# Attention with a soft mixture of experts: the guard of the row sums moved from VectorE into TensorE's accumulation

## The chip, the cores and the metric

The kernel runs on one core of a Trainium2 chip. Its engines are named as in the profile: PE (TensorE, with PEld for its weight loads), DVE (VectorE), ACT (ScalarE), POOL (GpSimd) and SP (SyncE, which issues the transfers). The metric is the device time of one execution in microseconds (us), the median of several runs.

## The reference

Four batches, eight heads, 768 positions, 64 values a head. Attention looks at the first 8 keys (global) and at a causal window of 96; a slope of its own for each head, times the distance, is subtracted. What follows is a soft mixture of eight experts with four slots each.

```python
scores = q @ k^T / 8 - slope[h] * dist          # masked to global or local keys
a = exp(scores - max); a = a / (a.sum(-1) + 1e-9)
x = (a @ v) as 3072 rows of 512
logits = x @ phi                                # 32 slots
d = softmax(logits over rows);  slot_input = d^T @ x
slot_out[e] = relu(slot_input[e] @ w1[e]) @ w2[e]
out = softmax(logits over slots) @ slot_out
```

## The kernel before, in words

The attention runs in 16 units (batch and pair of heads, i = 0 and 1 within the pair). The queries of a head are cut into seven blocks of 120, the last with 48. For a unit the steps are these, each named in the code:

- `scores` (PE, three parts) makes the scores of both heads in PSUM, fp32, keys on the partitions; `biased` (DVE, three parts) adds the bias table, writes the tile `tb` and keeps a running maximum `mx`.
- `max_t` (PE) turns that maximum, `max_r` (DVE) reduces it to `nb`; `exponential` (ACT) makes `exp(tb + nb)` in place.
- `w_hi` (ACT) rounds the weights to 16 bits into `ph`, `w_lo` (POOL, now and then DVE) puts what is left over beside them. `v_hi` (POOL or ACT) and `v_lo` (DVE) do the same for the values; `v_hi` has a further column of constants, so that column 64 of each block's product is the row sum.
- `values` (PE) multiplies: 39 products of 64 or 65 columns for a head, all into one PSUM bank `x`, seven blocks of 65 columns side by side. The first of the 39 starts the accumulation, the last ends it.
- `ev_sums` (DVE) adds a small guard `eps` to the 14 row sums of both heads and writes them into `rsall`; `ev_recs` (DVE) takes their reciprocals into `rc`; `ev_mul` (DVE, one for each head) multiplies the values by them into `xn` and so frees the bank. In `eps`, rows of the last block that hold no query have 1e30, so that their reciprocal is next to nothing. For the last unit `ev_sum` and `ev_rec` do this for one head.
- `tr` (PE) and `tr_copy` (ACT, sometimes DVE) turn the result, `logits` and the `strip_` steps, `by_token` and `dispatch` take it into the mixture of experts as the units come in, and every batch's sum into `sacc`.

The order of all steps is one list written out, `ORDER`, which every engine follows for its own instructions: an engine whose next instruction waits does nothing else meanwhile. The loads of the expert weights are steps of this list as well (`piece`, `extra`, `free`); SP issues them.

Ahead of the list stand constants: six filler products on PE, the first part of a bias table (`BiasTable`, POOL and DVE), memsets on POOL (`ones`, `v`, `ph`, `lsb`, `shift`, `eps`). The list then begins with loads, `bcast` (DVE casts the two sizes `nraw` to `nf`, PE spreads them over the partitions with `ones`), `keys` and the `table_` steps (DVE, later ACT), six fillers (`warm`, products of 512 columns whose result nobody reads) and the first `scores`.

Behind the list come the last dispatch, the experts' two layers (`hidden`, `project`) and the combination with its output, whose products PE does one after the other. Beside them `check_inputs` (DVE) tests among other things that the smallest row sum in `rsall` is large enough; if a test fails, a slow general version runs.

Of the kernel before, what the change touches and what calls it, by code (L numbers as in the profile page):

```python
# [10 lines left out]
F32 = mybir.dt.float32  # L11
# [12 lines left out]
KB = 120  # L24
P = 128
NJ = 7
# [28 lines left out]
NT = B * NJ  # L55
SW = 2 * KB
NEG = -1.0e30
V_SC = 2.0 ** 6
P_EXP = 15
RS_MIN = 2.0 ** (P_EXP + 6 - 10)  # L60
RS_EPS = 1.0e-9 * RS_MIN
X_MIN = 2.0 ** -9


T_SC = 0.125
TAB_UNIT = 0.5 / T_SC

# [233 lines left out]
def tile_attention_moe(ctx: ExitStack, tc: tile.TileContext, qk, v, phi, w1, w2, nn, out):  # L301
# [120 lines left out]
    def extra(i):  # L422
        if extras:
            k, c0, c1 = extras.pop(0)
            load_w([k], c0, c1)

    sacc = ap.tile([P, DM], F32, name="sacc")
    nraw = keep.tile([1, 4], I32, name="nraw")
    nc.scalar.dma_start(out=nraw, in_=nn)

    def load_phis(u):
        nc.sync.dma_start(out=phis, in_=phi)


    lnat = keep.tile([KB, 8 * B, NS], F32, name="lnat")
    xmax = keep.tile([KB, B * H], F32, name="xmax")
    rsall = keep.tile([KB, B * H, NJ], F32, name="rsall")
    state = keep.tile([P, 16], F32, name="state")
    sl = keep.tile([P, Moe.SL], F32, name="sl")
    lsb = ap.tile([P, SW], F32, name="lsb")  # L440
    ex = ap.tile([P, SW], F32, name="ex")
    i4 = keep.tile([P, NS], F32, name="i4")
    by_row = keep.tile([P, NS], F32, name="by_row")
    ones = keep.tile([P, P], F32, name="ones")

    def blocks(w):
        return w[:, 0:6 * PB].rearrange("p (s c) -> p s c", c=PB)


    wp = psm.tile([P, 512], F32, name="wp", tag="m")  # L450
    busy_in = nc.const_aps.tensor(1.0, [P, 512], BF16)
    for _ in range(WARM):
        nc.tensor.matmul(out=wp[0:1], lhsT=busy_in[:, 0:1], rhs=busy_in, start=True, stop=True)

    table = BiasTable(nc, tabs, xn01)
    nf = keep.tile([1, 4], F32, name="nf")
    nlt = keep.tile([P, 2], F32, name="nlt")
    nc.gpsimd.memset(ones, 1.0)
    make_identity(nc, ident)
    for i in range(2):  # L460
        nc.gpsimd.memset(vhi[i][:, :, :, D:D + 1], V_SC)
        for w in (phi_[i], plo_[i]):
            nc.gpsimd.memset(blocks(w)[:, :, QW:], 0.0)
            nc.gpsimd.memset(w[:, 6 * PB:], 0.0)
    nc.gpsimd.memset(lsb[96:128, :], NEG)

    def late_constants():
        nc.gpsimd.tensor_tensor(out=i4, in0=ident[:, 0:32], in1=ident[:, 32:64], op=ALU.add)
        nc.gpsimd.tensor_tensor(out=i4, in0=i4, in1=ident[:, 64:96], op=ALU.add)
        nc.gpsimd.tensor_tensor(out=i4, in0=i4, in1=ident[:, 96:128], op=ALU.add)  # L470
        nc.gpsimd.tensor_copy(out=by_row.rearrange("p (s j) -> p s j", s=4), in_=ident.rearrange("p (s r) -> p s r", s=4)[:, :, 0:NS // 4])
        nc.gpsimd.memset(sl, 0.0)
        moe.constants()

    shift = keep.tile([P, 1], F32, name="shift")
    nc.gpsimd.memset(shift, -P_EXP * float(np.log(2.0)) / T_SC)


    eps = keep.tile([KB, NJ], F32, name="eps")
    nc.gpsimd.memset(eps, RS_EPS)
    nc.gpsimd.memset(eps[:, NJ - 1:NJ], 1.0e30)
    nc.gpsimd.memset(eps[0:TN[6], NJ - 1:NJ], RS_EPS)
    nc.scalar.activation(out=state[0:1, 4:5], in_=nc.const_aps.tensor(1.0, [1, 1], F32), func=AF.Exp)


    sc = [pss.tile([P, 2, 512], F32, name=f"sc{k}", tag=f"sc{k}") for k in range(2)]
    xx = psx.tile([P, 2, 512], F32, name="x", tag="x")
    mxs, nbs, rcs, ms = {}, {}, {}, {}  # L490

    def tb(u):
        return tbuf[u % 3]
# [111 lines left out]
    def values(u, i):  # L605
        ph, pl = phi_[i], plo_[i]
        vh, vl = vhi[u % 2], vlo[u % 2]
        x = sums(u, i)
        ops = []
        for t in range(NJ):  # L610
            for j, c in ((t, PCOL[t]), (t - 1, PCOL[t - 1] + KB)):
                if j >= 0:
                    for w, vv, d in ((ph, vh, D + 1), (ph, vl, D), (pl, vh, D + 1)):
                        ops.append((t, c, w, vv, j, d))
        for z, (t, c, w, vv, j, d) in enumerate(ops):
            nc.tensor.matmul(out=x[:, (D + 1) * t:(D + 1) * t + d], lhsT=w[:, c:c + P], rhs=vv[:, j, i, 0:d],  # L616
                             start=(z == 0), stop=(z == len(ops) - 1), skip_group_check=True)

    xv = xx[0:KB, :, 0:NJ * (D + 1)].rearrange("p i (t d) -> p i t d", d=D + 1)

    def by_query(u, i):
        return sums(u, i)[0:KB, 0:NJ * (D + 1)].rearrange("p (t d) -> p t d", d=D + 1)

    def ev_sum(u, i):
        nc.vector.tensor_tensor(out=rsall[:, 2 * u + i, :], in0=by_query(u, i)[:, :, D], in1=eps, op=ALU.add)

    def ev_rec(u, i):
        rcs[u, i] = wk.tile([KB, NJ], F32, name="rc", tag="rc", bufs=3)
        nc.vector.reciprocal(out=rcs[u, i], in_=rsall[:, 2 * u + i, :])

    def ev_sums(u):
        nc.vector.tensor_tensor(out=rsall[:, 2 * u:2 * u + 2, :], in0=xv[:, :, :, D], in1=eps.unsqueeze(1).to_broadcast([KB, 2, NJ]), op=ALU.add)

    def ev_recs(u):
        rc = wk.tile([KB, 2, NJ], F32, name="rc", tag="rc", bufs=3)
        for i in range(2):
            rcs[u, i] = rc[:, i]
        nc.vector.reciprocal(out=rc, in_=rsall[:, 2 * u:2 * u + 2, :])

    def ev_mul(u, i):  # L640
        b, p = units[u]
        c = D * (2 * (p % 2) + i)
        m = 2 * u + i
        nc.vector.tensor_tensor_reduce(  # L644
            out=xnb[(u // 2) % 3][:, :, c:c + D], in0=by_query(u, i)[:, :, 0:D], in1=rcs.pop((u, i)).unsqueeze(2).to_broadcast([KB, NJ, D]), scale=1.0,
            scalar=-3.0e38, op0=ALU.mult, op1=ALU.max, accum_out=xmax[:, m:m + 1])
# [225 lines left out]
    def table_rest_act(u):  # L872
        table.rest(nc.scalar.copy)

    def table_pair_act(p):
        table.pair_act(p)

    def table_pair(p):
        table.pair(p)

    steps = dict(piece=piece_of, free=free, extra=extra, load_phis=load_phis, bcast=bcast, keys=keys, table_rest=table_rest, table_rest_act=table_rest_act, table_pair_act=table_pair_act, warm_x=warm_x, warm=warm,
                 table_even=table_even, table_odd=table_odd, table_pair=table_pair, load_qk=load_qk, load_v=load_v, v_hi=v_hi, v_hi_act=v_hi_act, v_hi_dve=v_hi_dve, v_lo=v_lo,
                 scores=scores, biased=biased, max_t=max_t, max_r=max_r, exponential=exponential, w_hi=w_hi, w_lo=w_lo, w_lo_dve=w_lo_dve, w_hi_dve=w_hi_dve,
                 values=values, ev_sum=ev_sum, ev_rec=ev_rec, ev_sums=ev_sums, ev_recs=ev_recs, ev_mul=ev_mul, tr=tr, tr_copy=tr_copy, tr_copy_dve=tr_copy_dve,
                 logits=logits, logits2=logits2, logits_half=logits_half, logits_all=logits_all, strip_max=strip_max, strip_exp=strip_exp,
                 strip_sum=strip_sum, by_token=by_token, by_token_copy=by_token_copy, lnat_copy=lnat_copy, dispatch=dispatch, dispatch_sum=dispatch_sum)
    late_constants()
    for name, u, *args in ORDER:
        steps[name](u, *args)
    left = LeftBanks()  # L890
    put_rest = last_dispatch(left, lambda: warm_x(last))
    att.close()


    tail = ExitStack()
    ts = tail.enter_context(tc.tile_pool(name="ts", bufs=1))
# [10 lines left out]
    def check_inputs():  # L907

        def reduced(c, rows, x, axes, at_least):
            nc.vector.tensor_reduce(out=fl[0:rows, c:c + 1], in_=x, axis=axes, op=ALU.min)  # L910
            nc.vector.tensor_scalar(out=fl[0:rows, c:c + 1], in0=fl[0:rows, c:c + 1], scalar1=at_least, scalar2=None, op0=ALU.is_ge)

        reduced(1, KB, rsall[:, :, 0:6], AX.XY, RS_MIN)
        reduced(6, TN[6], rsall[0:TN[6], :, 6], AX.X, RS_MIN)
        xt = left.tile([P, 512], F32, name="xt", tag="x")
        nc.tensor.transpose(out=xt[0:B * H, 0:KB], in_=xmax, identity=ident[0:KB, 0:KB])
        nc.vector.tensor_reduce(out=fl[0:B * H, 5:6], in_=xt[0:B * H, 0:KB], axis=AX.X, op=ALU.max)
        nc.vector.tensor_scalar(out=fl[0:B * H, 5:6], in0=fl[0:B * H, 5:6], scalar1=X_MIN, scalar2=None, op0=ALU.is_ge)
        reduced(7, KB, cst[:, :, 1], AX.X, 0.5)
# [300 lines left out]
```

## Time and profile before

| | us |
|---|---|
| median of three runs | 184.98 (184.78 to 185.03) |
| profiled execution | 185.42 |
| its span, first to last instruction | 183.3 |
| busy: PE, DVE, ACT, POOL | 170.7, 141.4, 125.7, 97.2 |

The profile is of one execution. Matmuls are pipelined and their ends are modelled, so a busy PE is not PE at its peak. A row of the timeline merges like instructions in sequence: start in us from the span's beginning, duration in us, engine, line, operation, output<-inputs, shape of one, count, and in brackets the idle time before it with what ended it. A row of the waits reads: engine, tile and line that waited, what it waited for, us in total, times, longest. A row on groups has busy us and mean ns of one behind the bar.

### The profile page before, as it was taken

What the parts mean: (1) busy time and instruction counts of PE and PEld (TensorE: products, weight loads), DVE (VectorE), ACT (ScalarE), POOL (GpSimd) and SP (SyncE); (2) the same over time, 40 slices, a digit from 0 to 9 for tenths busy, and PEclk for the clock granted to TensorE, in tenths of its full rate; (3) what the DMA queues carried; (4) which work ended last, traced back from release to release, by engine and by line L of the source; (5) the groups of instructions that cost most, each with busy time, mean ns of one, the idle gap of its engine ahead of it and who ended that gap; (6) DMA issues with size and microseconds to landing.
All of it is one profiled execution on the core that took longest, in us unless ns stands there. A gap on an engine that the chain in (4) does not pass through costs nothing.

```text
span 183.3 us, 6741 instructions
## 1 busy us (share of the span) xinstructions
PE 170.7 (93%) x2805; PEld 125.8 (69%) x2805; DVE 141.4 (77%) x376; ACT 125.7 (69%) x162; POOL 97.2 (53%) x129
## 2 busy tenths in 40 slices
PE   8999899999999999999999998999899999999720
PEld 2476789787878877979888986875533256778520
DVE  5899999999998989899999999987867303345430
ACT  3489989999989999988999999953302120344320
POOL 6925689859799498797998996750010000000000
PEclk9999999999999999999999999999999999999985
DMA  5999999968999956689887399999999999989792
GB/s 191 418 407 384 398 370 384 366 229 306 414 330 353 405 154 256 230 325 382 297 326 272 87 323 384 396 356 418 415 401 407 411 401 406 370 307 401 294 368 65
DMA packets 15306, 61.41 MB, mean 335 GB/s; under 512 B 1698, under 2 KB 2850, under 8 KB 13474
## 3 DMA queue, kind: packets, MB, share of 16 engines
q1 hardware_dynamic: 15264, 60.89, 87.9%
q8 instruction: 24, 0.39, 0.9%
q14 instruction: 16, 0.13, 0.2%
q10 hardware_dynamic: 2, 0.00, 0.0%
HBM read 54.59 MB, written 6.29 MB: 332 GB/s over the span
## 4 chain that ended last, share of the span: by engine, by line


## 5 line engine op out<-in xcount | busy, mean ns | idle before, releaser
L599 POOL TENSOR_TENSOR ph<-tb,ph 128x432 f16<-128x432 f32 x83 | 85.8, 1064 | 19.5 <-ACT ph L592 18.3
L589 ACT ACTIVATE tb<-tb,nb 128x1296 f32<-128x1296 f32 x32 | 43.7, 1375 | 1.4 <-DVE nb L585 1.4
L616 PEld LDWEIGHTS <-ph 128*128 128x128 f16 x1248 | 40.7, 97 | 4.2 <-issue 2.8
L592 ACT CAST ph<-tb 128x1296 f16<-128x1296 f32 x32 | 40.6, 1272 | 2.8 <-PE x L616 0.9
L616 PE MATMUL x<-v,ph 128*128 128x65 f16 (+1 forms) x1209 | 42.0, 193 | 0.4 <-POOL ph L599 0.2
L564 PE MATMUL sc<-raw 64*128 64x216 f32 (+1 forms) x392 | 40.9, 340 | 0.0
L564 PEld LDWEIGHTS sc<-raw 64*128 64x128 f32 x392 | 32.3, 186 | 6.3 <-issue 3.8
L644 DVE CUSTOM_DVE_ANT_1 xn<-x,rc 120x448 f32<-120x448 f32 x31 | 18.3, 622 | 2.1 <-PE m L767 1.7
L573 DVE CUSTOM_DVE_ANT_1 tb<-sc,tt,mx 128x864 f32<-128x864 f32 x16 | 17.8, 1114 | 1.1 <-DVE mx L573 0.5
L542 DVE SCALAR_TENSOR_TENSOR v<-vt,v 128x896 f16<-128x896 f32 x14 | 16.2, 1160 | 0.0
L656 PE MATMUL m<-ident,xn 120*128 120x120 f32 x98 | 14.7, 276 | 0.2 <-DVE state L737 0.2
L656 PEld LDWEIGHTS m<-ident,xn 120*128 120x128 f32 x98 | 10.0, 141 | 2.7 <-issue 1.5
L101 PE MATMUL hp<-wp,sl 128*32 128x512 f32 x80 | 10.9, 595 | 0.3 <-ACT sl L96 0.3
L599 DVE TENSOR_TENSOR ph<-tb,ph 128x432 f16<-128x432 f32 x13 | 9.6, 766 | 0.0
L208 PE MATMUL cp<-sos,ct 32*128 32x128 f32 (+1 forms) x116 | 8.2, 332 | 1.3 <-DVE sos L195 1.1
L573 DVE CUSTOM_DVE_ANT_1 tb<-sc,xtt,mx 128x864 f32<-128x864 f32 x8 | 8.9, 1115 | 0.4 <-DVE mx L573 0.2
L573 DVE CUSTOM_DVE_ANT_1 tb<-sc,xta,mx 128x864 f32<-128x864 f32 x8 | 8.9, 1111 | 0.2
L573 DVE CUSTOM_DVE_ANT_1 tb<-sc,tt 128x864 f32<-128x864 f32 x8 | 8.4, 1052 | 0.5 <-PE sc L564 0.4
L535 ACT ACTIVATE v<-vt 128x896 f16<-128x896 f32 x9 | 8.6, 952 | 0.1
L156 PE MATMUL o<-wp,ht 128*32 128x128 f32 x256 | 8.2, 275 | 0.0
L156 PEld LDWEIGHTS o<-wp,ht 128*32 128x32 f32 x256 | 6.6, 110 | 1.4 <-issue 1.0
L903 POOL MEMSET ht<- 128x536 f32 x1 | 0.5, 547 | 13.1 <-PE ld L841 13.1
(235 smaller groups left out, 284.6 us busy)
## 6 DMA issues: line engine op xcount, KB each, us to landing
raw<-in_qk_dram SPq DMA_DIRECT2D x14, 832.0 KB, 5.8
wp<-in_w_dram SPq DMA_DIRECT2D x10, 1024.0 KB, 8.3
wp<-in_w_dram SPq DMA_DIRECT2D x15, 512.0 KB, 9.0
vt<-in_v_dram SPq DMA_DIRECT2D x14, 448.0 KB, 5.2
tb<-in_w_dram SPq DMA_DIRECT2D x3, 1024.0 KB, 7.8
wp<-in_qk_dram SPq DMA_DIRECT2D x2, 832.0 KB, 9.5
raw<-in_w_dram SPq DMA_DIRECT2D x2, 832.0 KB, 4.6
ph<-in_w_dram SPq DMA_DIRECT2D x2, 768.0 KB, 9.6
```

Source lines behind the costliest of these rows:

```text
L101: self.nc.tensor.matmul(out=hp[n][32 * s:32 * s + 32, :], lhsT=slv(a, c, s), rhs=w1(4 * a + s, c // 2)[:, (c % 2) * DF + 512 * n:(c % 2) * ...
L156: nc.tensor.matmul(out=o[32 * s:32 * s + 32, o0:o0 + w], lhsT=ht[:, k:k + 32], rhs=w2(4 * a + s, half)[:, at:at + w], start=(a == 0 and c ...
L535: nc.scalar.activation(out=vhi[u % 2][:, :, :, 0:D], in_=vraws(u), func=AF.Copy, scale=V_SC)
L542: nc.vector.scalar_tensor_tensor(out=vlo[k].rearrange("p j i d -> p (j i) d"), in0=vraws(u).rearrange("p j i d -> p (j i) d"), scalar=V_SC ...
L564: nc.tensor.matmul(out=z[:, i, at:at + n], lhsT=r_[r, KCOL[j]:KCOL[j] + KR], rhs=r_[r, KW + KB * j:KW + KB * j + n], start=True, stop=True)
L573: nc.vector.tensor_tensor_reduce(out=tb(u)[:, :, BW * k:BW * k + BW], in0=sc[(3 * u + k) % 2][:, :, 0:BW], in1=table.unit(u % NP, k), scal ...
L589: nc.scalar.activation(out=t, in_=t, func=AF.Exp, bias=nbs[u], scale=T_SC)
L592: nc.scalar.copy(out=blocks(phi_[i])[:, :, 0:QW], in_=tb(u)[:, i].rearrange("p (s c) -> p s c", c=QW))
L599: (engine or nc.gpsimd).tensor_tensor(out=blocks(plo_[i])[:, c, 0:QW], in0=tb(u)[:, i].rearrange("p (s c) -> p s c", c=QW)[:, c], in1=bloc ...
L616: nc.tensor.matmul(out=x[:, (D + 1) * t:(D + 1) * t + d], lhsT=w[:, c:c + P], rhs=vv[:, j, i, 0:d], start=(z == 0), stop=(z == len(ops) - ...
L644: nc.vector.tensor_tensor_reduce(out=xnb[(u // 2) % 3][:, :, c:c + D], in0=by_query(u, i)[:, :, 0:D], in1=rcs.pop((u, i)).unsqueeze(2).to_ ...
L656: nc.tensor.transpose(out=m[:, at:at + KB], in_=xnb[(u // 2) % 3][:, t, P * (p % 2):P * (p % 2) + P], identity=ident[0:KB, 0:KB])
```

## The change

The guard is added by PE: after the first of a head's 39 products a further product goes into the same accumulation. Its weights `eps_to` (128x128, bf16) are ones, its moving operand `eps_of` (128x7, bf16) holds the guard as a sum of three bf16 numbers in rows 0, 32 and 64; row 96 holds 1e30 for the last block, with zeros in `eps_to` where that block has queries. Both tiles are made by seven memsets on DVE, in place of three on POOL for `eps`. `ev_sums` and `ev_sum` go; the reciprocals are taken from PSUM into `recs`, which stays for the test at the end: the largest reciprocal against a bound in place of the smallest sum.

```diff
-ORDER = [... ('piece', 4), ('ev_sums', 0), ('ev_recs', 0), ('max_t', 2), ('biased', 3, 0), ...
+ORDER = [... ('piece', 4), ('ev_recs', 0), ('max_t', 2), ('biased', 3, 0), ...
...
+def in_parts(x, n):
+    parts = []
+    for _ in range(n):
+        bits = np.float32(x).view(np.uint32)
+        parts.append(float((bits & np.uint32(0xffff0000)).view(np.float32)))
+        x = float(np.float32(x - parts[-1]))
+    return parts
+
+RS_EPS_PARTS = in_parts(float(np.float32(RS_EPS)), 3)
...
-    rsall = keep.tile([KB, B * H, NJ], F32, name="rsall")
+    recs = keep.tile([KB, B * H, NJ], F32, name="recs")
...
     nc.gpsimd.memset(ones, 1.0)
+    eps_to = keep.tile([P, P], BF16, name="eps_to")
+    eps_of = keep.tile([P, NJ], BF16, name="eps_of")
+    nc.vector.memset(eps_to, 1.0)
+    nc.vector.memset(eps_to[96:97, 0:TN[6]], 0.0)
+    nc.vector.memset(eps_of, 0.0)
+    for k, part in enumerate(RS_EPS_PARTS):
+        nc.vector.memset(eps_of[32 * k:32 * k + 1], part)
+    nc.vector.memset(eps_of[96:97, NJ - 1:NJ], 1.0e30)
     make_identity(nc, ident)
...
-    eps = keep.tile([KB, NJ], F32, name="eps")
-    nc.gpsimd.memset(eps, RS_EPS)
-    nc.gpsimd.memset(eps[:, NJ - 1:NJ], 1.0e30)
-    nc.gpsimd.memset(eps[0:TN[6], NJ - 1:NJ], RS_EPS)
...
             nc.tensor.matmul(out=x[:, (D + 1) * t:(D + 1) * t + d], lhsT=w[:, c:c + P], rhs=vv[:, j, i, 0:d],
                              start=(z == 0), stop=(z == len(ops) - 1), skip_group_check=True)
+            if z == 0:
+                nc.tensor.matmul(out=x[:, 0:NJ * (D + 1)].rearrange("p (t d) -> p t d", d=D + 1)[:, :, D], lhsT=eps_to, rhs=eps_of,
+                                 start=False, stop=False, skip_group_check=True)
...
-    def ev_sum(u, i):
-        nc.vector.tensor_tensor(out=rsall[:, 2 * u + i, :], in0=by_query(u, i)[:, :, D], in1=eps, op=ALU.add)
-
     def ev_rec(u, i):
-        rcs[u, i] = wk.tile([KB, NJ], F32, name="rc", tag="rc", bufs=3)
-        nc.vector.reciprocal(out=rcs[u, i], in_=rsall[:, 2 * u + i, :])
-
-    def ev_sums(u):
-        nc.vector.tensor_tensor(out=rsall[:, 2 * u:2 * u + 2, :], in0=xv[:, :, :, D], in1=eps.unsqueeze(1).to_broadcast([KB, 2, NJ]), op=ALU.add)
+        nc.vector.reciprocal(out=recs[:, 2 * u + i, :], in_=by_query(u, i)[:, :, D])
 
     def ev_recs(u):
...
-        nc.vector.reciprocal(out=rc, in_=rsall[:, 2 * u:2 * u + 2, :])
+        nc.vector.reciprocal(out=recs[:, 2 * u:2 * u + 2, :], in_=xv[:, :, :, D])
...
-        reduced(1, KB, rsall[:, :, 0:6], AX.XY, RS_MIN)
-        reduced(6, TN[6], rsall[0:TN[6], :, 6], AX.X, RS_MIN)
+        reduced(1, KB, recs[:, :, 0:6], AX.XY, 1.0 / RS_MIN, ALU.max, ALU.is_le)
+        reduced(6, TN[6], recs[0:TN[6], :, 6], AX.X, 1.0 / RS_MIN, ALU.max, ALU.is_le)
```

Apart from the fifteen `ev_sums` and the two `ev_sum` taken out, `ORDER` is the same list.

## Rows read from the trace of the kernel before

**Rows 1.** Busy time by stage, 40 to 60: PE, PEld, DVE, ACT, POOL (instructions).
```profile
40.00:60.00 20.00, 19.96 (x331) 16.43 (x329) 18.96 (x50) 18.80 (x22) 16.89 (x17) 1.00 0.94 353
```

**Rows 2.** Waits of PE, 8 to 118 us: total, times, longest.
```profile
PE m L580 <- DVE mx L573: 0.6, 1, 0.6
PE m L580 <- ACT xtt L661: 0.4, 1, 0.4
PE m L656 <- DVE state L737: 0.2, 1, 0.2
PE x L616 <- POOL ph L599: 0.2, 1, 0.2
```

**Rows 3.** Timeline of PE, groups of value products and what follows one.
```profile
33.60 1.36 PE L616 MATMUL x<-v,ph 128*128 128x65 f16 x39
34.80 0.30 PE L580 MATMUL m<-ident,mx 128*128 128x128 f32 x1
...
109.27 2.52 PE L616 MATMUL x<-v,ph 128*128 128x65 f16 x78
```

**Rows 4.** Timeline of DVE at the start: cast, sizes, first bias.
```profile
3.10 0.34 DVE L852 CAST nf<-nraw 1x4 f32<-1x4 int32 x1
4.18 0.16 DVE L858 TENSOR_SCALAR nlt<-m 128x2 f32<-128x2 f32 x1 [0.74 <-PE m L854]
...
7.67 1.06 DVE L573 CUSTOM_DVE_ANT_1 tb<-sc,tt 128x864 f32<-128x864 f32 x1 [0.42 <-PE sc L564]
```

**Rows 5.** Timeline of DVE at 22 us; of PE, two groups of scores.
```profile
21.95 0.16 DVE L632 TENSOR_TENSOR rsall<-x,eps 120x14 f32<-120x14 f32 x1
22.15 0.24 DVE L638 RECIPROCAL rc<-rsall 120x14 f32<-120x14 f32 x1
...
22.34 2.10 PE L564 MATMUL sc<-wp 64*128 64x216 f32 x20
...
84.97 1.87 PE L564 MATMUL sc<-raw 64*128 64x216 f32 x20
```

**Rows 6.** Timeline of POOL and PE, three places with a wait.
```profile
76.96 1.01 POOL L532 TENSOR_SCALAR v<-vt 128x896 f16<-128x896 f32 x1 [1.03 <-PE x L616]
...
97.37 0.65 PE L616 MATMUL x<-v,ph 128*128 128x65 f16 x16 [0.17 <-POOL ph L599]
...
111.88 0.94 POOL L532 TENSOR_SCALAR v<-vt 128x896 f16<-128x896 f32 x1 [1.79 <-PE x L616]
```

**Rows 7.** Groups of instructions of DVE: the sums with their guard.
```profile
L632 DVE TENSOR_TENSOR rsall<-x,eps 120x14 f32<-120x14 f32 x15 | 2.5, 167 | 0.6 <-PE x L616 0.4
```

**Rows 8.** Timeline of DVE and PE, last unit's evaluation and transpose.
```profile
124.40 0.62 DVE L644 CUSTOM_DVE_ANT_1 xn<-x,rc 120x448 f32<-120x448 f32 x1
...
125.52 0.63 PE L656 MATMUL x<-ident,xn 120*128 120x120 f32 x4
```

**Rows 9.** Timeline of PE, short products; L841's durations (ns, min/median/max).
```profile
131.96 0.61 PE L841 MATMUL ld<-zi,sacc 128*128 128x32 f32 x4
...
L841 PE MATMUL ld<-zi,sacc x8: 276/276/297, 132.0 to 134.2; 128*128 128x32 f32 x8
```

**Rows 10.** Timeline of POOL and PE: constant, broadcast, fillers early and later.
```profile
3.23 0.20 POOL L458 MEMSET ones<- 128x128 f32 x1
...
3.59 0.55 PE L854 MATMUL m<-nf,ones 1*128 1x4 f32 x2
4.07 2.62 PE L553 MATMUL x<-const-bfloat16-1.0 128*1 128x512 bf16 x6
...
13.41 1.25 PE L553 MATMUL x<-const-bfloat16-1.0 128*1 128x512 bf16 x5
```

**Rows 11.** Timeline of DVE, short operations.
```profile
134.72 0.07 DVE L935 MEMSET fl<- 128x12 f32 x1
...
153.15 0.14 DVE L921 TENSOR_SCALAR fl<-nv 128x1 f32<-128x1 f32 x1
153.21 0.14 DVE L922 TENSOR_SCALAR fl<-nv 128x1 f32<-128x1 f32 x1
```

More of the change, by code (lines that the diff above doesn't have):

```diff
@@ L489, in tile_attention_moe @@
     xx = psx.tile([P, 2, 512], F32, name="x", tag="x")
-    mxs, nbs, rcs, ms = {}, {}, {}, {}
+    mxs, nbs, ms = {}, {}, {}
     def tb(u):
@@ L622, in by_query @@
         return sums(u, i)[0:KB, 0:NJ * (D + 1)].rearrange("p (t d) -> p t d", d=D + 1)
-    def ev_sum(u, i):
-        nc.vector.tensor_tensor(out=rsall[:, 2 * u + i, :], in0=by_query(u, i)[:, :, D], in1=eps, op=ALU.add)
     def ev_rec(u, i):
-        rcs[u, i] = wk.tile([KB, NJ], F32, name="rc", tag="rc", bufs=3)
-        nc.vector.reciprocal(out=rcs[u, i], in_=rsall[:, 2 * u + i, :])
-    def ev_sums(u):
-        nc.vector.tensor_tensor(out=rsall[:, 2 * u:2 * u + 2, :], in0=xv[:, :, :, D], in1=eps.unsqueeze(1).to_broadcast([KB, 2, NJ]), op=ALU.add)
+        nc.vector.reciprocal(out=recs[:, 2 * u + i, :], in_=by_query(u, i)[:, :, D])
     def ev_recs(u):
-        rc = wk.tile([KB, 2, NJ], F32, name="rc", tag="rc", bufs=3)
-        for i in range(2):
-            rcs[u, i] = rc[:, i]
-        nc.vector.reciprocal(out=rc, in_=rsall[:, 2 * u:2 * u + 2, :])
+        nc.vector.reciprocal(out=recs[:, 2 * u:2 * u + 2, :], in_=xv[:, :, :, D])
     def ev_mul(u, i):
@@ L644, in ev_mul @@
         nc.vector.tensor_tensor_reduce(
-            out=xnb[(u // 2) % 3][:, :, c:c + D], in0=by_query(u, i)[:, :, 0:D], in1=rcs.pop((u, i)).unsqueeze(2).to_broadcast([KB, NJ, D]), scale=1.0,
+            out=xnb[(u // 2) % 3][:, :, c:c + D], in0=by_query(u, i)[:, :, 0:D], in1=recs[:, 2 * u + i].unsqueeze(2).to_broadcast([KB, NJ, D]), scale=1.0,
             scalar=-3.0e38, op0=ALU.mult, op1=ALU.max, accum_out=xmax[:, m:m + 1])
@@ L883, in tile_attention_moe @@
                  scores=scores, biased=biased, max_t=max_t, max_r=max_r, exponential=exponential, w_hi=w_hi, w_lo=w_lo, w_lo_dve=w_lo_dve, w_hi_dve=w_hi_dve,
-                 values=values, ev_sum=ev_sum, ev_rec=ev_rec, ev_sums=ev_sums, ev_recs=ev_recs, ev_mul=ev_mul, tr=tr, tr_copy=tr_copy, tr_copy_dve=tr_copy_dve,
+                 values=values, ev_rec=ev_rec, ev_recs=ev_recs, ev_mul=ev_mul, tr=tr, tr_copy=tr_copy, tr_copy_dve=tr_copy_dve,
                  logits=logits, logits2=logits2, logits_half=logits_half, logits_all=logits_all, strip_max=strip_max, strip_exp=strip_exp,
@@ L907, in check_inputs, with reduced @@
     def check_inputs():
-        def reduced(c, rows, x, axes, at_least):
-            nc.vector.tensor_reduce(out=fl[0:rows, c:c + 1], in_=x, axis=axes, op=ALU.min)
-            nc.vector.tensor_scalar(out=fl[0:rows, c:c + 1], in0=fl[0:rows, c:c + 1], scalar1=at_least, scalar2=None, op0=ALU.is_ge)
-        reduced(1, KB, rsall[:, :, 0:6], AX.XY, RS_MIN)
-        reduced(6, TN[6], rsall[0:TN[6], :, 6], AX.X, RS_MIN)
+        def reduced(c, rows, x, axes, bound, low=ALU.min, within=ALU.is_ge):
+            nc.vector.tensor_reduce(out=fl[0:rows, c:c + 1], in_=x, axis=axes, op=low)
+            nc.vector.tensor_scalar(out=fl[0:rows, c:c + 1], in0=fl[0:rows, c:c + 1], scalar1=bound, scalar2=None, op0=within)
+        reduced(1, KB, recs[:, :, 0:6], AX.XY, 1.0 / RS_MIN, ALU.max, ALU.is_le)
+        reduced(6, TN[6], recs[0:TN[6], :, 6], AX.X, 1.0 / RS_MIN, ALU.max, ALU.is_le)
         xt = left.tile([P, 512], F32, name="xt", tag="x")
```

2 lines of the change are left out of this document (1 added, 1 removed).

## The prediction

> **What bounds the kernel now.** I read the busy time by stage first. In 40 to 60 us PE, DVE, ACT and POOL are all above 16.8 of 20 us, PE's matmul row at 19.96, DVE at 18.96, ACT at 18.80 [rows 1]; busy shares alone name no bound. So I read who waits. Between 8 and 118 us PE waits four times, 1.4 us in all: 0.6 and 0.2 for DVE, 0.4 for ACT, 0.2 for POOL [rows 2]. The timeline of PE says the same from the other side: a head's 39 value products start at 33.60 and take 1.36, the next instruction starts at 34.80, inside the modelled end of the group [rows 3]. A busy matmul is not a matmul at its peak, but its start times aren't modelled: 78 products take 2.52 us where 39 take 1.36, so one pair of weight load and product costs (2.52 - 1.36)/39 = 0.030 us, in every group, with no gap between groups. From about 24 us to 77 us I therefore take PE to set the pace, with DVE close behind but not ahead.
>
> Other stretches are set by other engines, and I followed the waits from place to place. Before 22 us it is DVE: it begins the first bias at 7.67 after 0.42 of idle [rows 4] and then runs almost without a gap to 21.95, and the longest of PE's waits, 0.6 in front of the maximum's transpose at 22.08, is for it [rows 2]. At 76.96 POOL's conversion has waited 1.03 for PE's values, POOL then holds up ACT, and PE itself stops for POOL at 97.37 [rows 6]: from 77 to 97 the path runs over POOL and ACT. From 97.4 it is PE again until POOL, at 111.88, has waited 1.79 for its values [rows 6]. After that the path goes POOL, PE, ACT, PE, DVE into the mixture of experts, whose products follow one another on PE to the end; what is late at 127 us is late at the end.
>
> **The sums and their guard on DVE.** The fifteen `ev_sums` cost 0.167 each, 2.5 in all [rows 7]; with the gap to the dependent reciprocal each takes 0.20 of DVE's time (21.95 to 22.15 [rows 5]). Two `ev_sum` of the last unit, no longer than these, go as well: 17 x 0.20 = 3.4 us less for DVE. The reciprocal now reads the accumulator itself. `ev_sums` reads the same accumulator and eps in 0.167, so I put the reciprocal's change at nothing, with 0.1 each (1.7, hidden as far as DVE has the 3.4 to give) as the upper bound. Where does the 3.4 arrive? Only where someone waits for DVE just behind an `ev_sums`. That is one place: unit 0's, at 21.95, stands in front of `biased(3,0)`, and the 20 score products at 22.34 take 2.10 where 20 elsewhere (84.97) take 1.87 [rows 5]. That 0.2 comes back. In the last unit the product `ev_mul(15,0)` starts on DVE at 124.40 and takes 0.62, but PE transposes it only at 125.52 [rows 8], behind other products in its queue: 0.5 us of slack, so both `ev_sum` there are worth nothing. Bounds: 0 to 0.6 (three such places).
>
> **The guard on PE.** Each of 32 heads gets one weight load of 128x128 16-bit values and one product of seven columns. No row has this pair. The nearest is the value product itself, with a weight load of the same size: 0.030 [rows 3]. From below it could be next to nothing, if load and product slip in beside their neighbours; from above, four fp32 products of 32 columns with 128x128 fp32 weights take 0.61 where one lasts 0.276, so (0.61 - 0.276)/3 = 0.11 apiece [rows 9]. I take 0.030, since both operands are 16-bit and the columns are fewer than 64. Not all 32 are on the path: unit 0's two lie before PE's wait at 22.08; units 1 to 8 are 16 heads in the stretch 24 to 77; the next six fall where PE waits for POOL and ACT; about four count in 97 to 112; in the last units the added product is second in a group that then waits anyway. So 20 x 0.030 = 0.6 us (0 to 2.2 by the bounds).
>
> [...]
>
> **The constants at the start.** Three POOL memsets go, into the shade of POOL's other constants. Seven DVE memsets come, and where they stand counts: in program order behind the bias table's first part and ahead of the cast of `nf`. That cast starts at 3.10 and takes 0.34 [rows 4]; `ones` on POOL ends at 3.23 + 0.20; PE's broadcast starts at 3.59 [rows 10]. So both operands are there at 3.43 and 3.44: the cast has no slack. Behind it wait the broadcast, then six fillers on PE in order (4.07 + 2.62), the first scores, and on DVE, from 4.18, the rest of the bias table [rows 4, 10]. Everything up to the DVE-paced stretch moves by what the memsets take. A memset lasts 0.07 [rows 11]; independent small operations start 0.06 apart (153.15, 153.21 [rows 11]); one that must wait for its predecessor's write starts 0.20 behind it, as the reciprocal does. Two of the seven overwrite part of the preceding one. The first is 128 columns wide, perhaps 0.1 more. So 5 x 0.06 + 2 x 0.20 = 0.7, between 0.4 (all at 0.06) and 1.4 (all at 0.20). I take 0.7.
>
> **The sum.** +0.7 at the start, -0.2 at 22 us, +0.6 on PE: +1.1 us. The check at the end reduces a tile of the same size (one maximum for one minimum) while PE works on products, at nothing. The profiled execution took 185.42, of which 183.3 is the span and 2.1 lies around it; that is 0.44 above the median of the three runs, 184.98. All terms are differences, so I put them on the median: 186.1 us. What a measurement here can tell from no change is about 0.2%, 0.37 us.
>
> **Rivals.**
> *DVE sets the pace after all (faster).* For: DVE is at 18.96 of 20 [rows 1], and it is relieved by 3.4 us. Against: in all these 110 us PE waits only 0.8 for DVE, 0.6 of it at 22 us [rows 2]. If each removed sum counted, the time would be 184.98 + 0.7 - 3.4 + (products now in the shade) 0 = 182.3. It decides from the point where more than six of the 17 places reach the path, since 0.7 + 0.6 is what stands against them. [...] Chance 0.11.
> *Start hidden, gain found (same).* The memsets fit in 0.4, and DVE's lead shortens a few of PE's late waits, half of the 0.8 behind 22 us [rows 2]: 0.4 - 0.2 - 0.4 + 0.5 = +0.3, 185.3. For: the small cost of an independent operation [rows 11]. Against: of PE's waits behind 22 us 0.6 are for ACT and POOL and only 0.2 for DVE. Chance 0.12.
> *The product is dear.* At 0.11 apiece 20 x 0.11 = 2.2, sum +2.7: 187.7. Against it stands the pair's 0.030. Chance 0.06.
> *The clock rises later.* [...] Chance 0.08.
>
> **How the numbers follow.** The forecast itself has 0.63, with its own range from 185.4 (memsets 0.4, gain 0.4, product 0.4) to 187.0 (memsets 1.2, gain 0, product 0.8). With the dear product and the late clock, slower by over 0.2% has 0.77; same 0.12; faster 0.11. A range from 185.0 to 187.6 leaves out the DVE-paced case and the dear product, together with the edges under 0.2.
>
> **What would show it.** Right: the cast of `nf` starts some 0.7 later than 3.10, the first bias at about 8.4; PE's group at 22.34 loses its 0.2; a head's group of 40 products takes 1.39 instead of 1.36; DVE is relieved by about 3 us and shows it as longer waits for PE, not as an earlier end. Wrong: the cast starts at 3.2, or the mixture of experts starts earlier than before although PE has more to do; then DVE, or something it releases, was the pace, and my reading of PE's gapless starts is the step that failed. A weight load of more than 0.1 visible as a gap behind the seven columns would fail the price of the product; a filler at 0.43 after 7 us would show the clock.

## The result, and the profile after

The kernel after takes 187.63 us (median of 4 runs, 187.51 to 187.78), the kernel before, run beside it, 184.88 (184.33 to 185.03): a ratio of 1.0138, with a 95% interval from 1.0111 to 1.0165, or +2.75 us. The forecast was 186.1 with a range to 187.6: the direction is right, and the time lies just past the upper end. The profiled execution took 187.68, of which 185.6 is the span and 2.1 lies around it; before it was 183.3 and 2.1. So the two traces have +2.3 between their spans to explain.

The timeline of the kernel after at its start: DVE, then POOL beside it, then PE to the turn of the first and of the third maximum.

```profile
3.15 0.17 DVE L476 MEMSET eps_to<- 128x128 bf16 x1
...
3.94 0.06 DVE L481 MEMSET eps_of<- 1x1 bf16 x1
4.03 1.14 DVE L864 CAST nf<-nraw 1x4 f32<-1x4 int32 x1
5.91 0.16 DVE L870 TENSOR_SCALAR nlt<-m 128x2 f32<-128x2 f32 x1 [0.74 <-PE m L866]
...
7.36 1.47 DVE L284 SCALAR_TENSOR_TENSOR tt<-xn 128x216 bf16<-128x216 f32 x2
...
9.95 1.06 DVE L592 CUSTOM_DVE_ANT_1 tb<-sc,tt 128x864 f32<-128x864 f32 x1 [0.25 <-PE sc L583]
...
3.88 0.16 POOL L484 MEMSET v<- 128x14 f16 x1
3.92 0.28 POOL L486 MEMSET ph<- 128x192 f16 x1
...
5.01 0.14 POOL L487 MEMSET ph<- 128x48 f16 x1
5.21 0.29 POOL L488 MEMSET lsb<- 32x240 f32 x1
...
7.51 1.09 POOL L551 TENSOR_SCALAR v<-vt 128x896 f16<-128x896 f32 x1
...
5.32 0.55 PE L866 MATMUL m<-nf,ones 1*128 1x4 f32 x2 [1.83 <-DVE nf L864]
5.80 2.72 PE L572 MATMUL x<-const-bfloat16-1.0 128*1 128x512 bf16 x6
8.45 2.18 PE L583 MATMUL sc<-raw 64*128 64x216 f32 x16
...
13.71 0.29 PE L599 MATMUL m<-ident,mx 128*128 128x128 f32 x1
...
24.35 0.32 PE L599 MATMUL m<-ident,mx 128*128 128x128 f32 x1 [0.52 <-DVE mx L592]
24.61 1.90 PE L583 MATMUL sc<-wp 64*128 64x216 f32 x20
```

In the kernel before, the first scores and the turn of the first maximum stand at:

```profile
6.63 1.73 PE L564 MATMUL sc<-raw 64*128 64x216 f32 x16
...
11.44 0.29 PE L580 MATMUL m<-ident,mx 128*128 128x128 f32 x1
```

Read from the left. The cast stood at 3.10 and took 0.34 [rows 4]; now it stands at 4.03, since the memsets take 0.93, and takes 1.14. Four numbers are cast, as before. PE's broadcast is at 5.32 instead of 3.59 [rows 10], the fillers take 2.72, 0.43 each, to 8.5 us, and 16 score products take 2.18 instead of 1.73. The first bias is 2.28 late, and the first maximum is turned at 13.71 instead of 11.44, 2.27 late. From there to the end of the span are 171.9 us in both kernels: all of the +2.3 is there at 14 us, and everything behind it gives and takes nothing in the sum.

Behind the start, three steps of the forecast can be read directly. The waits of PE between 8 and 121 us:

```profile
PE m L599 <- DVE mx L592: 0.5, 1, 0.5
PE m L599 <- ACT xtt L673: 0.4, 1, 0.4
PE x L635 <- POOL ph L618: 0.4, 1, 0.4
```

PE's timeline for one head with its added product, and behind it two rows of the same head in the kernel before:

```profile
33.04 0.20 PE L635 MATMUL x<-v,ph 128*128 128x65 f16 x1
33.07 0.17 PE L638 MATMUL x<-eps_of,eps_to 128*128 128x7 bf16 x1
33.10 1.30 PE L635 MATMUL x<-v,ph 128*128 128x64 f16 x38
34.24 0.60 PE L668 MATMUL m<-ident,xn 120*128 120x120 f32 x4
```

```profile
30.95 1.34 PE L616 MATMUL x<-v,ph 128*128 128x65 f16 x39
32.13 0.61 PE L656 MATMUL m<-ident,xn 120*128 120x120 f32 x4
```

And the group of DVE's reciprocals (busy us, mean ns of one, idle time before them):

```profile
L650 DVE RECIPROCAL recs<-x 120x14 f32<-120x14 f32 x15 | 3.6, 241 | 0.5 <-PE x L635 0.4
```

PE's wait for DVE's state [rows 2] is gone, the one for POOL has grown from 0.2 to 0.4. The score group behind the third maximum takes 1.90 instead of 2.10 [rows 5]. The head's 40 products take 34.24 - 33.04 = 1.20, where its 39 took 32.13 - 30.95 = 1.18: 0.02 for the added one. The reciprocal from PSUM takes 0.241, no more than the one from SBUF [rows 5].

### The profile page after: what moved, and what is told of

The parts are those of the page before. It is cut to its first block, busy times and chain, and to the rows that moved or that the text cites. A ratio compares the mean times of both kernels' runs of the same rounds, so it can differ in the third digit from the quotient of the medians.

```text
span 185.6 us, 6792 instructions
## 1 busy us (share of the span) xinstructions
PE 171.6 (92%) x2837; PEld 127.0 (68%) x2837; DVE 142.2 (77%) x366; ACT 125.6 (68%) x162; POOL 97.0 (52%) x126
## 4 chain that ended last, share of the span: by engine, by line
## 5 line engine op out<-in xcount | busy, mean ns | idle before, releaser
L635 PE MATMUL x<-v,ph 128*128 128x65 f16 (+1 forms) x1209 | 42.8, 193 | 0.5 <-POOL ph L618 0.4
L656 DVE CUSTOM_DVE_ANT_1 xn<-x,recs 120x448 f32<-120x448 f32 x31 | 18.3, 621 | 2.4 <-PE m L779 2.0
```

The costliest lines, as they stand in the source:

```text
L656: nc.vector.tensor_tensor_reduce(out=xnb[(u // 2) % 3][:, :, c:c + D], in0=by_query(u, i)[:, :, 0:D], in1=recs[:, 2 * u + i].unsqueeze(2). ...
```

## Experiments

The first theory from the two traces (theory 1): POOL's chain of memsets, which runs without a gap from 3.88 to 5.15, holds up DVE's cast, and later POOL work the table. Its plain form (theory 1b): only that DVE is late counts, whatever PE does. The rival (theory 2): the start would be absorbed, and the added products make the time. Theory 3 came out of the first results: behind PE's pause ahead of the broadcast (1.83 us without an instruction) PE goes over later from a pace at which a filler takes 0.43 to one at which it takes 0.22. The expectations call this the rise of the clock. That it is a clock was my reading and isn't shown: the traces show the pace, and a granted clock of 1.00 through the first 60 us in both kernels.

Ratios are to runs of the kernel before on the same chip. "First maximum" is where PE begins to turn it, in the profiled execution.

| run | cast (us) | PE idle before broadcast | six fillers | 16 scores | first maximum | span | median, ratio (95%) |
|---|---|---|---|---|---|---|---|
| before | 0.34 | | 2.62 | 1.73 | 11.44 | 183.3 | |
| after | 1.14 | 1.83 | 2.72 | 2.18 | 13.71 | 185.6 | 187.63, 1.0138 (1.0111 to 1.0165) |
| after, again | 1.14 | 1.83 | 1.47 | 1.73 | 12.99 | 185.3 | 187.33, 1.0147 (1.0095 to 1.0200) |
| constants on POOL | 0.34 | | 1.65 | 1.73 | 10.92 | 182.6 | 185.00, 1.0001 (0.9977 to 1.0025) |
| memsets behind the cast | 0.35 | | 1.47 | 1.73 | 11.07 | 183.0 | 185.17, 0.9999 (0.9981 to 1.0018) |
| before + memsets | 0.18 | 0.87 | 2.72 | 2.90 | 13.40 | 185.2 | 187.49, 1.0135 (1.0106 to 1.0163) |
| POOL clear | 0.26 | 0.95 | 2.72 | 2.07 | 12.73 | 184.6 | 187.38, 1.0119 (1.0090 to 1.0148) |
| more fillers | 1.14 | 0.73 | 1.46 | 1.73 | 12.99 | 184.7 | 186.98, 1.0108 (1.0075 to 1.0141) |
| POOL clear, more fillers | 0.26 | | 2.09 | 1.73 | 12.37 | 184.3 | 186.48, 1.0051 (1.0028 to 1.0074) |
| before + memsets, more fillers | 0.79 | 0.62 | 1.46 | 1.73 | 12.80 | 184.9 | 187.57, 1.0120 (1.0095 to 1.0145) |
| before, fewer fillers | 0.34 | 0.95 | 2.72 | 2.06 | 11.86 | 183.4 | 186.93, 1.0113 (1.0071 to 1.0155) |
| the same, again | 0.35 | 0.95 | 2.72 | 3.25 | 13.01 | 185.8 | 187.92 (one run) |

### Where the memsets stand

The seven memsets of the kernel after, on POOL, where the three old ones were:

```diff
-    nc.vector.memset(eps_to, 1.0)
...
-    nc.vector.memset(eps_of[96:97, NJ - 1:NJ], 1.0e30)
...
     nc.gpsimd.memset(shift, -P_EXP * float(np.log(2.0)) / T_SC)
+    nc.gpsimd.memset(eps_to, 1.0)
...
+    nc.gpsimd.memset(eps_of[96:97, NJ - 1:NJ], 1.0e30)
```

> The kernel after, with the seven constants of the guard written by POOL, behind shift, where the three old ones stood; the product, the reciprocals and the check stay. Theory 1 (the loss is the start: the cast of nf begins 0.93 late and then takes 1.14 in place of 0.34, the table behind it is slower): the cast is back at 3.1 with 0.34, the first bias near 7.7, and what is left is the product at 16 x 0.015 = +0.24 less the 0.2 at 22 us: 184.9 to 185.3. Theory 2 (the start's loss would be absorbed later, the product or the slower reciprocal on DVE makes the time): 186.3 or more.

185.00, ratio 1.0001. The cast is back at 3.10 with 0.34 and PE's broadcast at 3.59. Theory 2 is refuted: with all 32 products in place the loss is gone.

The memsets on DVE, but right behind the cast of `nf`:

```diff
...
     nc.vector.tensor_copy(out=nf, in_=nraw)
+    nc.vector.memset(eps_to, 1.0)
...
+    nc.vector.memset(eps_of[96:97, NJ - 1:NJ], 1.0e30)
```

> The kernel after, with the seven DVE memsets right behind the cast of nf, where DVE waits 0.74 for PE's broadcast. Theory 1: the cast is back at 3.1 with 0.34; the memsets take some 0.85 of which 0.74 is idle time, so the first bias comes 0.1 to 0.5 late: 185.1 to 185.6. If the memsets cost their length wherever they stand, or slow POOL's constants: 186 or more. Theory 2 (product): 186.3 or more.

185.17, ratio 0.9999. The seven fall into DVE's wait for PE's broadcast; the first maximum is at 11.07. Not even the 0.1 to 0.5 that I had allowed for is left: where the memsets are put is the whole of the loss.

The kernel before with the same seven memsets, and nothing else:

```diff
...
     nc.gpsimd.memset(ones, 1.0)
+    eps_to = keep.tile([P, P], BF16, name="eps_to")
+    nc.vector.memset(eps_to, 1.0)
...
+    nc.vector.memset(eps_of[96:97, NJ - 1:NJ], 1.0e30)
     make_identity(nc, ident)
```

> The kernel before, with the same seven memsets on DVE at the same place, into two tiles that nobody reads; nothing else is changed. Theory 1 (the memsets push the cast and the table's two-operand sums into the time in which POOL writes its own constants, and beside those they run slower): the cast starts at 4.0 and takes 1.1, first bias near 9.9, +2.3 in all: 187.0 to 187.4. A mere shift by the memsets' own 0.9: 185.8. Theory 2 (the loss is the product's): 185.0 to 185.8.

187.49, ratio 1.0135: the memsets alone bring the whole loss, as theory 1 had it, but not in its way. The timeline, DVE, POOL and PE:

```profile
4.03 0.18 DVE L871 CAST nf<-nraw 1x4 f32<-1x4 int32 x1
4.96 0.16 DVE L877 TENSOR_SCALAR nlt<-m 128x2 f32<-128x2 f32 x1 [0.74 <-PE m L873]
...
9.36 1.06 DVE L592 CUSTOM_DVE_ANT_1 tb<-sc,tt 128x864 f32<-128x864 f32 x1 [1.31 <-PE sc L583]
...
3.88 0.16 POOL L480 MEMSET v<- 128x14 f16 x1
3.92 0.28 POOL L482 MEMSET ph<- 128x192 f16 x1
...
4.36 0.56 PE L873 MATMUL m<-nf,ones 1*128 1x4 f32 x2 [0.87 <-DVE nf L871]
4.85 2.72 PE L572 MATMUL x<-const-bfloat16-1.0 128*1 128x512 bf16 x6
7.50 2.90 PE L583 MATMUL sc<-raw 64*128 64x216 f32 x16
```

The cast starts at the same hundredth, POOL's memsets stand where they did to within 0.02, and here it takes 0.18. DVE has its table ready 1.31 before PE has scores for it: the 16 score products take 2.90 instead of 1.73. This DVE is 0.8 late (ready at 9.36 less 1.31, 8.05, against 7.25 before), the first maximum 1.96 and the kernel, by its ratio, 2.5. What decides here is PE, at half its pace.

POOL's memsets of `v`, `ph` and `lsb` moved behind the second `v_hi`, DVE's left where they are:

```diff
-    for i in range(2):
-        nc.gpsimd.memset(vhi[i][:, :, :, D:D + 1], V_SC)
...
-    nc.gpsimd.memset(lsb[96:128, :], NEG)
+    def pool_constants():
+        for i in range(2):
+            nc.gpsimd.memset(vhi[i][:, :, :, D:D + 1], V_SC)
...
+        nc.gpsimd.memset(lsb[96:128, :], NEG)
...
     def v_hi(u):
         nc.gpsimd.tensor_scalar(out=vhi[u % 2][:, :, :, 0:D], in0=vraws(u), scalar1=V_SC, scalar2=0.0, op0=ALU.mult, op1=ALU.add)
+        if u == 1:
+            pool_constants()
```

> The kernel after; the seven memsets stay on DVE ahead of the cast, but POOL's constants for v, ph and lsb move behind the second v_hi, so that POOL writes nothing while the cast runs. Theory 1 (POOL's writes hold up DVE's cast): the cast starts at 4.0 and takes 0.35 or less, the first bias at about 8.6 to 9.1, total 185.9 to 186.5. Rival (the cast is slow for another reason, such as the memsets' own writes or its own input arriving): it takes 1.1 again, total 187.3 to 187.8.

The cast takes 0.26:

```profile
4.03 0.25 POOL L493 TENSOR_TENSOR i<-ident 128x32 f32<-128x32 f32 x1
4.03 0.26 DVE L868 CAST nf<-nraw 1x4 f32<-1x4 int32 x1
```

So it is POOL's chain that holds it in the kernel after; here it ends 0.01 behind the POOL instruction that now stands beside it. But the time is 187.38, ratio 1.0119, where theory 1 expected at most 186.5. PE still pauses for 0.95, the fillers take 0.43 each, and the table's L284 takes 1.48, as in the kernel after. Theory 1 is right on the cast and doesn't explain the time.

### The pause of PE

The kernel before with four fillers ahead of everything in place of six, so that PE has less to do and pauses 0.95 ahead of the broadcast:

```diff
-WARM = 6
+WARM = 4
```

> The kernel before with four filler products in place of six at the very start; DVE and POOL are untouched. PE then ends at about 2.6 and stands idle for 0.9 ahead of the broadcast at 3.59, as it did for 0.87 in the kernel before with the seven memsets. [...] Theory 1b (what costs is only DVE's late start): 185.1, no change.

186.93, ratio 1.0113: theory 1b is refuted, since DVE and POOL are untouched to 7 us; theory 3 had put it at 186.5 to 187.4. The executions spread from 185.43 to 188.29, and the profile fell on the fastest. A second profile of the same kernel:

> [...] Theory 3: where the clock rises later, more of the first scores run at 0.36 a pair and the first bias comes later by as much, with DVE's table unmoved: 186.5 to 188.

PE and DVE of this second one:

```profile
3.59 0.56 PE L854 MATMUL m<-nf,ones 1*128 1x4 f32 x2 [0.95 <-POOL ident masks.py:197]
4.08 2.72 PE L553 MATMUL x<-const-bfloat16-1.0 128*1 128x512 bf16 x6
6.72 3.25 PE L564 MATMUL sc<-raw 64*128 64x216 f32 x16
...
13.01 0.32 PE L580 MATMUL m<-ident,mx 128*128 128x128 f32 x1
...
3.10 0.35 DVE L852 CAST nf<-nraw 1x4 f32<-1x4 int32 x1
...
8.58 1.06 DVE L573 CUSTOM_DVE_ANT_1 tb<-sc,tt 128x864 f32<-128x864 f32 x1 [1.34 <-PE sc L564]
```

The 16 scores take 3.25 instead of 2.06 in the first profile, almost all at half pace, and the first maximum comes at 13.01 instead of 11.86, with DVE's table as early as ever. Of the 2.4 between the two spans 1.15 is this. Most of the rest has nothing to do with the start: from the start of the last copy of the output to the end of the span the first profile needs 6.85, the second 8.42 (7.0 to 7.8 in all others), and SP's last output issue takes 2.42 instead of 0.87; why, no run shows. So how much of the 1.1% in time is the start's isn't settled: it is 0.4 and 1.6 us in the two profiles.

The kernel after with ten fillers in place of six:

```diff
-WARM = 6
+WARM = 10
```

> The kernel after with ten filler products in place of six at the very start, so that PE is busy to about 5.0 while DVE writes the seven constants and casts. Theory 3: there is no pause of more than 0.4, the clock rises by 6.5 as in the kernel before, the scores run at 0.18 a pair, and only the shift of DVE is left: 185.4 to 186.4. Theory 1b: PE's broadcast comes no earlier, so 187.4 or more.

186.98, ratio 1.0108: a miss for both. PE was early at the faster pace (six fillers in 1.46, scores in 1.73) and so in time, but the cast took 1.14 again, and the first bias came at 9.24 without a wait for PE. And the kernel after once more, unchanged:

> The kernel after once more, unchanged, for a second profile of it. If the cast's 1.14 is what costs, it is there again; if it is chance, the cast takes 0.2 to 0.35 here, PE starts its fillers near 4.9, and the time is still 187.5 (theory 3: the clock rises between 8 and 10 us in both).

The cast is at 1.14 again, not by chance, while PE is at the faster pace from 5.60 on this time. The timeline, PE, DVE and POOL:

```profile
5.60 1.47 PE L572 MATMUL x<-const-bfloat16-1.0 128*1 128x512 bf16 x6
6.99 1.73 PE L583 MATMUL sc<-raw 64*128 64x216 f32 x16
...
12.99 0.29 PE L599 MATMUL m<-ident,mx 128*128 128x128 f32 x1
...
8.18 1.14 DVE L293 COPY tt<-tt 128x432 bf16<-128x432 bf16 x3
9.24 1.05 DVE L592 CUSTOM_DVE_ANT_1 tb<-sc,tt 128x864 f32<-128x864 f32 x1
...
8.00 0.95 POOL L551 TENSOR_SCALAR v<-vt 128x896 f16<-128x896 f32 x1
```

So there are two ways from the memsets to the first maximum: over DVE (late cast, held cast, held table), which made +1.7 to +2.2 in the two kernels with more fillers whose profiles show the faster pace early (the second follows below), and over PE (a pause, then half pace), which with DVE as early as ever made 0.4 and 1.6 at the first maximum and +1.7 in the median time. That would be why neither cure by itself brought the time back. The test of that takes both away: POOL's constants behind the second `v_hi`, as above, and eight fillers.

```diff
-WARM = 6
+WARM = 8
```

> The kernel after with the memsets left on DVE, POOL's constants for v, ph and lsb moved behind the second v_hi, and eight fillers in place of six: neither POOL's hold on the cast nor a pause of PE is left. Theory 3 (both the hold and the late clock cost, and the later of the two decides): cast 0.26 at 4.03, clock by 6.5, first bias near 8.2, 185.9 to 186.5. If either alone is not the cause, 187.3 as with six fillers.

186.48, ratio 1.0051, at the upper end of theory 3's range. The loss falls from ratios of 1.0138 and 1.0147 (+2.5 and +2.7) to 1.0051 (+0.95), where taking away one of the two left 1.0108 and 1.0119 (+2.0 and +2.2). The rest is DVE again: 0.93 of memsets, and L284 at 1.54 instead of 0.80 beside POOL's `v_hi`, which now starts at 6.31.

Eight fillers, too, in the kernel before with the memsets, whose cast had taken 0.18:

> The kernel before with the seven memsets of DVE ahead of the cast (into tiles nobody reads), and eight filler products in place of six at the very start, so that PE works to 4.1 and waits only some 0.2 for the cast. In the same kernel with six fillers the cast took 0.18, and the time was +2.3. [...] Theory 1b (DVE's late start alone makes 2.3): 187.4 again.

187.57, ratio 1.0120, where theory 3 had 186.0 to 186.5: missed, and not a test of what I meant, since here the cast took 0.79 and PE paused for 0.62 after all. The cast and the POOL row whose end (4.80) it follows:

```profile
4.02 0.79 DVE L871 CAST nf<-nraw 1x4 f32<-1x4 int32 x1
...
4.53 0.27 POOL L482 MEMSET ph<- 128x192 f16 x1
```

With the same POOL rows to within 0.02 us the cast has now taken 0.18, 0.79 and 1.14; the first maximum follows at 12.80, with the six fillers in 1.46 and the scores in 1.73.

### The product and the sums

The kernel before with the product alone, its moving operand zero; `ev_sums` keeps the guard:

```diff
...
             if z == 0:
+                nc.tensor.matmul(out=x[:, 0:NJ * (D + 1)].rearrange("p (t d) -> p t d", d=D + 1)[:, :, D], lhsT=eps_to, rhs=eps_of,
+                                 start=False, stop=False, skip_group_check=True)
```

> The kernel before with the added product alone: its moving operand is zero, both constants are written by POOL, ev_sums with its guard stays on DVE. So the sums are the same. Theory 1 (a product costs 0.015): 16 to 20 of them are on the path, +0.2 to +0.3: 185.1 to 185.3. The price as forecast, 0.030: +0.6, 185.5. A dear product at 0.11: 187.

185.29, ratio 1.0008 (0.9989 to 1.0028): between nothing and +0.5; the dear product is excluded, the other two prices aren't told apart.

With the constants on POOL, three more products a head with a zero operand:

```diff
...
+                for _ in range(3):
+                    nc.tensor.matmul(out=x[:, 0:NJ * (D + 1)].rearrange("p (t d) -> p t d", d=D + 1)[:, :, D], lhsT=eps_to, rhs=eps_no,
+                                     start=False, stop=False, skip_group_check=True)
```

> The kernel after with the constants on POOL, and three more products a head, with a zero moving operand, so that the result is the same. The difference to the run with the constants on POOL is three times the price of the product where it is on the path: at 0.015 x 3 x 20 = +0.9; at 0.030, +1.8; if PE's pace were not the bound, 0.

186.89 (ratio 1.0100, 1.0076 to 1.0125) against 185.00 with one: 1.89 us for 96 products. Both traces turn the first maximum at 10.92; the whole difference arises behind it, 0.7 of it by 62 us. The same head with one added product and with four:

```profile
23.71 0.19 PE L635 MATMUL x<-v,ph 128*128 128x65 f16 x1
...
24.90 0.60 PE L668 MATMUL m<-ident,xn 120*128 120x120 f32 x4
```

```profile
23.71 0.19 PE L637 MATMUL x<-v,ph 128*128 128x65 f16 x1
...
24.98 0.61 PE L673 MATMUL m<-ident,xn 120*128 120x120 f32 x4
```

It becomes 0.08 longer by three products. From the start of a head's products to the start of PE's next instruction, 25 of the 32 heads are 0.07 to 0.08 longer, 0.025 a product; the other seven, where PE waits anyway (unit 0's second head, four heads between 87 and 98 us, the last two), change by -0.08 to +0.03. That is 25 x 0.075 = 1.9, the difference of the times. PE's pace is the bound, and the forecast's 0.030 x 20 = 0.6 agrees with 0.025 x 25 = 0.63.

The kernel after without the product and its constants (`w` are the two weight tiles of POOL's memsets, `phi_` those that hold the rounded weights):

```diff
...
-            nc.gpsimd.memset(w[:, 6 * PB:], 0.0)
+            nc.gpsimd.memset(w[:, 6 * PB:], 1.0 if w is phi_[i] else 0.0)
...
-            if z == 0:
-                nc.tensor.matmul(out=x[:, 0:NJ * (D + 1)].rearrange("p (t d) -> p t d", d=D + 1)[:, :, D], lhsT=eps_to, rhs=eps_of,
-                                 start=False, stop=False, skip_group_check=True)
```

> The kernel after without the product and its constants: the reciprocals are taken of the raw sums. It leaves out the guard of 1e-9; a column of weights is set to 1 in place of 0 in the last block's empty places, so that their sums aren't zero. What it tells is what ev_sums cost the kernel before. Theory 1: 0.2 at 22 us and little else: 184.4 to 184.8. Rival (DVE sets the pace): 182 or less.

184.83, ratio 0.9978 (0.9962 to 0.9995): the `ev_sums` were worth 0.4 (0.1 to 0.7). This is the one kernel faster than both, and it leaves out the guard; the rival that DVE sets the pace needed 182. With POOL's constants moved as well:

> As the run without the guard (which it leaves out as that one does), and POOL's constants for v, ph and lsb move behind the second v_hi. If POOL's writes slow the table on DVE at the start of the kernel before as well, the first bias comes before 7.67 and the whole by as much: 184.0 to 184.5. If DVE's start waits for POOL's table and the loads anyway: no difference to the run without the guard; slower where POOL's constants now delay the first w_lo.

185.29, ratio 1.0005 (0.9983 to 1.0026), nothing gained: the sizes come 0.16 earlier, but the table's copies take 1.14 beside `v_hi`.

Last, the constants on POOL and three fillers in place of six between broadcast and scores:

```diff
-ORDER = [... ('table_even', 0), ('warm', 0, 6), ('scores', 0, 0), ...
+ORDER = [... ('table_even', 0), ('warm', 0, 3), ('scores', 0, 0), ...
...
```

> The kernel after with the constants on POOL, and three in place of six fillers between the broadcast and the first scores. If the clock rises once PE has been kept busy without a pause, by fillers or by scores alike, the scores start up to 1.3 earlier and DVE's first bias no longer waits 0.4 for them: 184.5 to 184.9, with less spread. If the fillers are needed for the rise, the scores stay at half pace: 185.5 or more.

185.90, ratio 1.0028 (1.0000 to 1.0057), with executions from 184.6 to 186.6: not faster. PE now waits 0.35 for the load of q and k ahead of the scores. Six of twelve executions lie at 186.25 or more, where with six fillers one of twelve does. In the one profile (with the 16 first scores in 1.73) the first maximum is turned at 10.92, as with six, and the 0.8 between the two spans arises behind it. So the run doesn't test whether PE gets to its faster pace behind scores as well as behind fillers; why it is no faster stays open.

## Why the forecast fell short

**The step that failed** is the one on the constants at the start: "Everything up to the DVE-paced stretch moves by what the memsets take", put at 0.7. The memsets took 0.93, inside the bounds of 0.4 to 1.4. But what stands behind them doesn't just move. The cast in its new place is held by POOL's chain for up to 0.9 (1.14 against 0.26), the table for some 0.6 more (L284 0.80 to 1.47 in one profile, L293 1.14 in the other), and behind PE's pause of 1.83 fillers and first scores took 2.72 and 2.18 in one profile, 1.47 and 1.73 in the other. In the profiled execution both ways came out nearly together: DVE was ready at 9.70 (9.95 less 0.25 of waiting), PE at 9.95; before, DVE was ready at 7.25 and PE at 7.67 [rows 4]. The start cost 2.27, not 0.7.

A row had the hint: the cast of four numbers took 0.34 in the kernel before [rows 4], with POOL writing `ones` until 3.43 [rows 10], and ended 0.01 behind that. I took 0.34 for its length; no run takes that write away.

In all its lengths the cast ends 0.01 to 0.02 behind the end of a POOL instruction. A wait for one such instruction would have been at most 0.28 here; the traces show that the cast can last to the end of a chain without gaps: 1.14 from 4.03, beside memsets that run from 3.88 to 5.15. At which end it gets in no run explains: it took 0.18 in one kernel, 1.14 in another, with the same rows to within 0.02. L284 took 1.48 and 1.54 beside `v_hi`, 0.80 without.

**The rival of the late clock** had 0.08, and the sign named for it is in the first trace: a filler at 0.43 after 7 us, where later ones take 0.22 [rows 10]. That a clock is behind it no run shows; the granted one stands at 1.00. PE's slower pace was one of two causes. My estimate of its price, 1.3, lies between what the pause alone cost at the first maximum in two profiles, 0.4 and 1.6 (11.86 and 13.01 against 11.44); that it comes out between them is chance, since the moment of the faster pace differs between executions. What my cases lacked is that DVE's way costs as much by itself, so that the loss stays when the faster pace comes early (first maximum at 12.99, ratio 1.0147).

**PE sets the pace from 24 us, DVE does not:** right. Three more products a head cost 1.89 us; taking the 17 sums from DVE (3.4 us by the forecast's count) gave 0.4 (0.1 to 0.7).

**The gain at 22 us:** right, 2.10 to 1.90, 0.2.

**The product:** right, and the working with it: 0.025 apiece in 25 heads and nothing in seven, 0.63, where 0.030 in 20 heads was forecast, 0.6. **Product and sums together:** forecast +0.4, measured with the start put right 0.0 (-0.4 to +0.5).

**The reciprocal from PSUM, the check, the last unit's sums at nothing:** right for the reciprocal (0.241); the others can't be seen apart in a remainder of 171.9 in both kernels.

## What to carry to other kernels

Ahead of the first stretch that keeps all engines busy, an instruction that is put in front of a small cast or copy may cost far more than its own length (here 0.93 of memsets made 2.27 at the first maximum): look which POOL work the moved instruction will now meet, and how long PE will stand without work. A small DVE operation that takes longer than its elements explain (0.34 for four) may be held already. And constants belong where their engine waits anyway: the same seven memsets, moved behind the cast, cost nothing (ratio 0.9999).

## What the runs showed of the hardware that was not expected

- A cast of 1x4 on DVE took 0.18, 0.26, 0.34, 0.79 or 1.14 us, and each time it ended 0.01 to 0.02 behind the end of a POOL instruction: at 4.21 (4.20), 4.29 (4.28), 3.44 (3.43), 4.81 (4.80) and 5.17 (5.15, the last memset of the chain, 5.01 + 0.14). Within the chain POOL's instructions end 0.07 to 0.2 apart, so that one such agreement alone would say little.
- The moment at which PE goes from 0.43 to 0.22 us a filler differs between executions of one kernel: in the kernel after, fillers at 0.43 to 8.5 us and the scores behind them in 2.18 in one profile, all six fillers from 5.60 on in 1.47 in another. So it lies behind 8.5 us in the one and ahead of 5.6 in the other. In all nine profiles without a pause of more than 0.3 ahead of the broadcast the 16 first scores take 1.73; with a pause of 0.6 to 1.8 they took longer in five of eight. The granted clock of these stretches is shown as 1.00 in both kernels; the pace is seen only in the products' durations.
